# Expert tiles: each 128x128 transpose becomes two on the row halves of the array, in two PSUM banks, with the banks shared out anew

## The chip, the cores and the metric

The kernel runs on one core of a Trainium2 chip. The metric is the device time of one execution in microseconds (us). TensorE is called PE here (PEld is its weight load), VectorE DVE, ScalarE ACT, GpSimd POOL.

## The reference

Three layers follow one another, all in fp32:

```python
# 1. attention with a memory: B, H, S, D = 4, 8, 576, 64
x = (g * mem_out + (1 - g) * softmax(causal(q k^T / 8)) v)      # rows x become 2304 x 512
# 2. top-1 mixture of experts: E = 8, F = 1024
expert = argmax(x @ w_gate);  p = softmax(x @ w_gate)[expert]
x = p * (relu(x @ w1[expert]) @ w2[expert])                      # 512 -> 1024 -> 512
# 3. feed-forward layer
out = elu(x @ w_in) @ w_out                                      # 512 -> 2048 -> 512
```

## The kernel before

The program has three phases: attention, the expert tiles, and the last layer. In each phase operations are recorded in a plan (`Plan.op`, with a cost, a priority and what is read and written); `Plan.order` then simulates the engines with those costs and writes out a fixed order for each engine. So the order on the chip does not react to what really happens: each engine takes its instructions in the written order, and waits where one isn't ready.

Matmuls are done in fp32r, with each operand split into a high and a low part: three matmuls (high by high, low by high, high by low) stand for one. `split` makes the parts: a cast (`hi`, L1208 on ACT or L1211 on DVE) and a subtraction (`lo`, L1214 on DVE).

The expert phase (`moe`) works on tiles of 128 tokens, sorted by expert; 23 tiles run with this data. For each tile:

- the rows are gathered by a DMA of POOL (tile `xg` or `ex`, asked for early), and four transposes of 128x128 (L1277) put them with the features on the partitions, into one PSUM bank of ring `t`; every fourth column is taken (`sg.t[:, cc:DM:4]`). `split` makes `xh` and `xl` (or `x`, the same in the other buffer) from the bank. I call these four transposes an X group.
- 24 matmuls (L1337) with the first weights fill two banks of ring `g`, and two relus (L1347) empty them into `h`.
- two groups of four transposes (L1362), one for each half of `h`, go to two banks of ring `t`, and `split` makes `hh` and `hl` from each. These are the H groups.
- 24 matmuls (L1380) sum the tile's output in the bank of ring `y`; the result is scaled (L1393) and scattered to DRAM.

Two early tiles also have a group of transposes of their result (L1411, Y group). PSUM has eight banks: ring `g` has 4, `t` 3 and `y` 1. A bank of ring `t` is handed out again when the subtraction that reads it last (L1214) has ended.

When the next tile belongs to another expert, its weights must be split too: ACT casts 8 blocks of 128x1024 (L1313) and DVE subtracts 8 (L1318). These stand in every tile's order behind a branch on a flag (L1311, L1316), and are skipped where the expert stays the same. The plan gives them one cost (`m_if`, 700 ns for a pair) whether they are skipped or not. In the gaps, ACT and DVE also prepare the last layer's weights (L1127 on ACT; L1131, L1135, L1139, L1143 on DVE), with loads and stores of their own.

Of the kernel before, what the change touches and what calls it, by code (L numbers as in the profile page):

```python
# [18 lines left out]
P = 128  # L19
B, H, S, D = 4, 8, 576, 64  # L20
DM = H * D
# [59 lines left out]

class Op:
    __slots__ = ("eng", "cost", "fn", "prio", "lat", "need", "users", "slots", "ready", "start", "seq", "why", "dma", "lag", "waits", "dense", "span", "mode")


class Plan:
# [364 lines left out]
def ca(n, sb=False, bias=False, acc=False):  # L451
    if acc:
        return 240 + 0.833 * n
    return (110 if sb else 65) + 0.833 * n


def cv(n):
    return 70 + 1.04 * n


def cv2(n):
    return 75 + 0.52 * n
# [6 lines left out]
def cpt(n):  # L469
    return 150 + 2.1 * n  # L470
# [733 lines left out]
def split(c, src, hi, lo, n, rd, wh, wl, pr, psum, eh, el):  # L1204
    nc, pl = c.nc, c.pl

    def ha():
        nc.scalar.copy(hi(), src())  # L1208

    def hv():  # L1210
        nc.vector.tensor_copy(hi(), src())  # L1211

    def lv():
        nc.vector.tensor_sub(lo(), src(), hi().bitcast(F32))  # L1214

    def lp():
        nc.gpsimd.tensor_sub(lo(), src(), hi().bitcast(F32))
    he = {"ACT": (ca(n, sb=not psum), ha), "DVE": (cv(n) if psum else cv2(n), hv)}
    le = {"DVE": (cv(n), lv), "POOL": (cpt(n), lp)}
    for es, d, r, w in ((eh, he, rd, wh), (el, le, rd + [wh], wl)):  # L1220
        pl.op(es, [d[x][0] for x in es], [d[x][1] for x in es], r=r, w=[w], prio=pr)


def moe(tc, c, w1, w2, tiles):
    nc = tc.nc
    mp, pl, K = c.mp, c.pl, c.K
# [28 lines left out]
    def mtile(t):  # L1255
        pr = 1000.0 * t
# [3 lines left out]
        sg = Slot(r_xg)  # L1260
        if t:
            for j in range(2):
                if t == 1 and j == 1:

                    def f():
                        for w in raw[2:]:
                            nc.gpsimd.memset(w[0:1, 0:1], 0.0)
# [5 lines left out]
        wx, xh, xl = Slot(rt), Slot(r_xh), Slot(r_xl)  # L1273

        def f():
            for cc in range(4):
                nc.tensor.transpose(wx.t[:, cc * P:(cc + 1) * P], sg.t[:, cc:DM:4], c.ident)  # L1277
        if t:
            pl.op("PE", 436, f, r=[sg], w=[wx], prio=pr + K["m_x"])
        else:  # L1280
            xh.index, xl.index = r_xh.free.pop(0)[1], r_xl.free.pop(0)[1]
        for _ in range(t > 0):
            split(c, lambda: wx.t, lambda: xh.t.rearrange("p c n -> p (c n)"), lambda: xl.t.rearrange("p c n -> p (c n)"), 512,
                  [wx], xh, xl, pr + K["m_x"], True, K["xe"], ("DVE",))

        flags = {}
        for e, eng in (("ACT", mybir.EngineType.Activation), ("DVE", mybir.EngineType.DVE)) if t else ():
            def mk(e, eng):
                n = t - NE if part else t

                def f():
                    flags[e] = nc.values_load(c.R.sw[part][0:1, 1, n:n + 1], engines=[eng], min_val=0, max_val=1,
                                              skip_runtime_bounds_check_because="made on the chip as a flag")
                pl.op(e, 450, f, r=[("sw", part)], w=[("flag", e, t)], prio=pr + K["m_fl"])
# [29 lines left out]
        g = [Slot(rg), Slot(rg)]  # L1324
# [18 lines left out]
        sh = Slot(r_h)  # L1343
# [12 lines left out]
        for k in range(2):  # L1356
            def mk(k):
                wt, hh, hl = Slot(rt), Slot(r_hh), Slot(r_hl)

                def f():  # L1360
                    for j in range(4):
                        nc.tensor.transpose(wt.t[:, j * P:(j + 1) * P], sh.t[:, (4 * k + j) * P:(4 * k + j + 1) * P], c.ident)  # L1362
                pl.op("PE", 436, f, r=[(sh, k)], w=[wt], prio=pr + K["m_h"])
                split(c, lambda: wt.t, lambda: hh.t.rearrange("p c n -> p (c n)"), lambda: hl.t.rearrange("p c n -> p (c n)"), 512,
                      [wt], hh, hl, pr + K["m_h"], True, K["he"], ("DVE",))
                hs.append((hh, hl))
            mk(k)

        y, sy = Slot(ry), Slot(Ring("last", [c.wraw[0][0][:, 2 * XW:3 * XW]]) if t == NTM - 1 else r_y)
# [34 lines left out]
        if t < NE:  # L1404
            wy = Slot(rt)
            n = P * (t - NE + NY)
            yh, yl = [lambda x=x: c.y0.t[:, x, 4 * n:4 * (n + P)] for x in range(2)]

            def f():
                for cc in range(4):  # L1410
                    nc.tensor.transpose(wy.t[:, cc * P:(cc + 1) * P], sy.t[:, cc * P:(cc + 1) * P], c.ident)  # L1411
            pl.op("PE", 436, f, r=[sy, "y0"], w=[wy], prio=pr + 500)
            split(c, lambda: wy.t, yh, yl, 512, [wy], ("yh", n), ("yl", n), pr + 500, True,
                  K["he"], ("DVE",))
            return

# [10 lines left out]
    for t in tiles:  # L1427
        mtile(t)
# [217 lines left out]
def kernel(ctx, tc, q, k, v, M_prev, z_prev, beta, w_gate, w1, w2, w_in, w_out, out):  # L1646
    nc = tc.nc
    c = Ctx()
# [8 lines left out]
    def psum(stack, name, n, two=0):  # L1657
        pp = stack.enter_context(tc.tile_pool(name=name, bufs=1, space=bass.MemoryType.PSUM))
        return [pp.tile([P, 512], F32, name=f"{name}{i}") for i in range(n)], [pp.tile([P, 1024], F32, name=f"{name}t{i}") for i in range(two)]
# [30 lines left out]
    with ExitStack() as s1:  # L1690
        c.wraw = [[wp.tile([P, 2048], F32, name=f"wraw{i}", tag=f"wraw{i}") for i in range(4)]]
        ep = s1.enter_context(tc.tile_pool(name="ep", bufs=1))
        c.x0 = [ep.tile([P, 4, P], F32R, name=f"x0{i}") for i in range(2)]
        c.wq = [[ep.tile([P, 1024], F32R, name=f"wq{n}{i}") for i in range(2)] for n in range(1)]
        with ExitStack() as s2:
            c.ap = s2.enter_context(tc.tile_pool(name="ap", bufs=1))
            c.qone = c.ap.tile([P, NI, 2 * QH], BF16, name="qone")
            c.ap.tile([P, (-8800 % LINE) // 4], F32, name="apad")
            nx = c.K["rings"]
            banks, twos = psum(s2, "pa", 8 - 2 * nx, nx)  # L1700
            c.rx = Ring("x", twos)
            c.rw = Ring("w", banks) if banks else c.rx
            c.rs = c.rw

            def build():
                constants(tc, ctx, c, M_prev, z_prev, beta, w_gate)
                attention(tc, ctx, c, q, k, v, M_prev)
                routing(tc, c, c.rw, True, c.K["early"])
                for j in range(2):
                    tile_weights(tc, c, (w1, w2), 0, j, prio=c.K["early"], dma=5830)  # L1710
                gather(tc, c, 0, lambda: c.ex[:, 0:XW], r=[("tok", 0)] + [("xd", b) for b in range(B - 1)], w=[c.se], prio=c.K["early"])
                first_parts(c)
                n, t0, dt = c.K["warm"]
                keep_busy(c, c.rw, [t0 + dt * i for i in range(n)], 1.0e8)
                wd = Widen.inside(tc, c, w_in, w_out)
                for n in range(c.K["wa"]):
                    wd.part(n, c.K["wa0"] + c.K["wa1"] * n)
            phase(build, c.K["sa"], 0.0, POOL=3000.0, DVE=1800.0, ACT=500.0, PE=2000.0)
        with ExitStack() as s2:
            c.mt = {}  # L1720
            c.mp = s2.enter_context(tc.tile_pool(name="mp", bufs=1))
            c.qone = c.mp.tile([P, NI, 2 * QH], BF16, name="qone")
            c.mp.tile([P, (-1440 % LINE) // 4], F32, name="mpad")
            c.wraw.append([c.mp.tile([P, 2048], F32, name=f"wrbw{i}") for i in range(4)])
            banks, _ = psum(s2, "pm", 8)
            c.rg, c.rt, c.ry = Ring("g", banks[:4]), Ring("t", banks[4:7]), Ring("y", banks[7:])
            
            def build():
                c.wd = Widen.inside(tc, c, w_in, w_out)
                keep_busy(c, c.rg, [0.0] * c.K["busy"][1], -1.0e8)  # L1730
                c.gate(c.rt, c.K["late"])
                routing(tc, c, c.rt, False, c.K["late"])
                moe(tc, c, w1, w2, range(NTM))
                for i, n in enumerate(range(c.K["wa"], 4 * NS)):
                    c.wd.part(n, 1.0e7 + 1.0e4 * i, r=[("tile", c.K["wt"] + int(i * c.K["wq"]))])
            phase(build, c.K["sm"])

            nt = nc.values_load(c.R.nt[0:1, 0:1], min_val=0, max_val=NT, skip_runtime_bounds_check_because="made on the chip as a count of tiles")
            with tc.If(nt > NTM):
                phase(lambda: moe(tc, c, w1, w2, range(NTM, NT)), c.K["sm"])  # L1740
    with ExitStack() as s1:
        c.tp = s1.enter_context(tc.tile_pool(name="tp", bufs=1))
        banks, _ = psum(s1, "pt", 8)
# [35 lines left out]
```

## Time and profile before

| | |
|---|---|
| median of 3 runs | 955.74 us (953.25 to 956.02) |
| profiled execution | 954.44 us, its span 952.7 us |
| PE busy in the span | 921.3 us (97%) |
| DVE, ACT, POOL busy | 639.2, 446.9, 179.6 us |
| granted clock of PE, mean | 0.991 |
| attention, experts, last layer | 0 to about 243, to 538, to 953 us |

A matmul's record is longer than the time it costs, since matmuls overlap in the array: "390 ns" of a matmul with 512 columns says little, while the distance from its start to the start of the next one, 0.23 us, is its price where PE is the bound. All prices of PE below are such distances.

### The profile page before, as it was taken

The numbers are of one execution on the slowest core, as the hardware profiler recorded it, in microseconds if no ns is written. First come the engines' busy times: TensorE is split into PE (matmuls) and PEld (weight loads), VectorE is DVE, ScalarE is ACT, GpSimd is POOL, SyncE is SP. The second block draws the span as 40 slices with busy tenths as digits, with TensorE's granted clock in tenths as the row PEclk, the third lists the DMA queues.
The fourth block names the chain that finished last, engine by engine and source line by source line (L and its number), as shares of the span: only waits on it lengthen the run. The fifth ranks groups of instructions, "written<-read, shape, count | busy, mean of one in ns | idle before, by whom it ended". The sixth has DMA issues, their size and how long they took to land. (4 is left out here: it accounts for less than half of the span.)

```text
span 952.7 us, 18441 instructions
## 1 busy us (share of the span) xinstructions
PE 921.3 (97%) x6858; PEld 770.3 (81%) x6858; DVE 639.2 (67%) x1179; ACT 446.9 (47%) x902; POOL 179.6 (19%) x244
## 2 busy tenths in 40 slices
PE   9998998999899999999999999999999999999996
PEld 6777887778678888888878789988888888888895
DVE  3878878887775568646898596555565556555553
ACT  3787778767454347536866562222122221212211
POOL 3344442434300122222321100010001000100100
PEclk8999999989999999999999999999999999999999
DMA  6333433243632697569997370110011000100000
GB/s 124 79 75 84 94 75 103 64 147 132 221 122 88 228 343 250 170 225 361 331 335 279 125 242 1 34 45 1 1 45 45 1 12 23 45 0 1 20 26 23
DMA packets 96597, 110.00 MB, mean 115 GB/s; under 512 B 64879, under 2 KB 64879, under 8 KB 94193
## 3 DMA queue, kind: packets, MB, share of 16 engines
q1 hardware_dynamic: 90496, 95.25, 31.4%
q0 software_dynamic: 4800, 13.18, 3.8%
q8 instruction: 55, 0.90, 0.4%
q10 hardware_dynamic: 1200, 0.30, 0.2%
q14 instruction: 46, 0.37, 0.1%
HBM read 87.94 MB, written 23.41 MB: 117 GB/s over the span
## 5 line engine op out<-in xcount | busy, mean ns | idle before, releaser
L1588 ACT ACTIVATE elu<-pt 128x512 f32<-128x512 f32 x72 | 43.1, 598 | 266.0 <-PE pt L1580 266.0
L1613 PE MATMUL pt<-w,gh 128*128 128x512 f32 x432 | 134.2, 392 | 0.5 <-DVE gh L1492 0.5
L1380 PE MATMUL pm<-w,hh 128*128 128x512 f32 x368 | 125.1, 401 | 0.8 <-ACT y L1393 0.8
L1596 DVE TENSOR_SCALAR elu<-elu 128x512 f32<-128x512 f32 x72 | 30.8, 428 | 127.1 <-ACT elu L1588 127.1
L1613 PEld LDWEIGHTS pt<-w,gh 128*128 128x128 f32 x432 | 79.6, 188 | 16.3 <-DVE gh L1492 0.9
L692 ACT ACTIVATE a<-pat,st 128x128 f32<-128x128 f32 (+2 forms) x144 | 78.0, 550 | 22.5 <-DVE st L687 18.3
L1613 PE MATMUL pt<-w,gl 128*128 128x512 f32 x216 | 84.3, 390 | 0.0
L1380 PEld LDWEIGHTS pm<-w,hh 128*128 128x128 f32 x368 | 69.2, 188 | 14.5 <-ACT y L1393 1.2
L1380 PE MATMUL pm<-w,hl 128*128 128x512 f32 x184 | 71.9, 391 | 0.3 <-DVE hl L1214 0.3
L687 DVE TENSOR_REDUCE st<-pat 128x2 f32<-128x256 f32 (+4 forms) x80 | 63.8, 806 | 9.6 <-PE pat L671 9.6
L1580 PE MATMUL pt<-yTh,w 128*128 128x256 f32 (+1 forms) x288 | 69.2, 319 | 0.0
L705 PE MATMUL pat<-ident,a 128*128 128x128 f32 x400 | 56.9, 287 | 8.6 <-ACT a L692 8.4
L628 POOL TENSOR_SCALAR ex<-ex 128x512 f32<-128x512 f32 (+1 forms) x32 | 37.8, 1182 | 131.0 <-ACT ex L604 118.5
L705 PEld LDWEIGHTS pat<-ident,a 128*128 128x128 f32 x400 | 44.6, 145 | 16.0 <-ACT a L692 15.0
L1600 DVE SCALAR_TENSOR_TENSOR tnh<-tnh,elu 128x512 f32<-128x512 f32 x72 | 49.6, 690 | 7.7 <-ACT tnh L1592 1.8
L1337 PE MATMUL pm<-w,x 128*128 128x512 f32 x216 | 51.9, 392 | 1.3 <-DVE w L1214 0.9
L1495 DVE TENSOR_TENSOR gl<-tnh,gh 128x512 fp32r<-128x512 f32 x72 | 49.6, 691 | 4.2
L1580 PEld LDWEIGHTS pt<-yTh,w 128*128 128x128 f32 x288 | 49.2, 190 | 4.0
L1604 DVE SCALAR_TENSOR_TENSOR tnh<-pt,tnh 128x512 f32<-128x512 f32 x72 | 49.6, 690 | 3.3
L1337 PEld LDWEIGHTS pm<-w,x 128*128 128x128 f32 x216 | 40.2, 188 | 10.3 <-DVE w L1214 1.4
L1214 DVE TENSOR_TENSOR hl<-pm,hh 128x512 fp32r<-128x512 f32 x46 | 31.4, 684 | 25.0 <-ACTq L1311 14.4
L1613 PEld LDWEIGHTS pt<-w,gl 128*128 128x128 f32 x216 | 40.5, 188 | 9.0 <-DVE gl L1495 0.4
(342 smaller groups left out, 2107.3 us busy)
## 6 DMA issues: line engine op xcount, KB each, us to landing
wraw<-in_moe_w_dram SPq DMA_DIRECT2D x24, 1024.0 KB, 7.9
wrbw<-in_moe_w_dram SPq DMA_DIRECT2D x12, 1024.0 KB, 8.1
wide<-in_moe_w_in_dram SPq DMA_DIRECT2D x16, 512.0 KB, 5.4
wf<-half SPq DMA_DIRECT2D x32, 256.0 KB, 3.2
wide<-in_moe_w_out_dram SPq DMA_DIRECT2D x16, 512.0 KB, 5.8
wide<-wf SPq DMA_DIRECT2D x9, 512.0 KB, 5.3
q<-in_q_dram SPq DMA_DIRECT2D x32, 128.0 KB, 3.1
v<-in_v_dram SPq DMA_DIRECT2D x32, 128.0 KB, 2.5
```

The lines of the kernel that those rows point to most:

```text
L628: nc.gpsimd.tensor_scalar(e, e, 1.0, 0.0, op0=ALU.min, op1=ALU.add)
L687: nc.vector.tensor_reduce(ss.t[:, 2 * i:2 * i + (2 if i < 4 else 1)], src(), axis=AX.X if i < 4 else AX.XY, op=ALU.min)
L692: nc.scalar.activation(sa[i].t[:, h, :] if i < 4 else sa[4].t[:, 0:S].rearrange("p (y n) -> p y n", y=2), src()[:, h, :] if i < 4 else src ...
L705: nc.tensor.transpose(w.t[:, y:y + P], t[:, j * P:(j + 1) * P], c.ident)
L1337: nc.tensor.matmul(g[hf].t, a.t[:, cc, :], b[:, 512 * hf:512 * (hf + 1)], start=(cc == 0 and n == 0), stop=(cc == 3 and n == 2))
L1380: nc.tensor.matmul(y.t, a.t[:, 2 * (q % 2) + jj, :], b[:, 512 * jj:512 * (jj + 1)], start=(q == 0 and jj == 0 and n == 0), stop=(q == 3 an ...
L1495: nc.vector.tensor_sub(lo(), src(), hi().bitcast(F32))
L1580: nc.tensor.matmul(h.t[:, n * j + n0:n * j + n1], w(cc, a, ft), b(cc), start=(cc == 0 and x == 0), stop=(cc == 3 and x == 2))
L1588: nc.scalar.activation(se.t, h.t, AF.Exp)
L1600: nc.vector.scalar_tensor_tensor(st.t, st.t, 0.0, se.t, op0=ALU.min, op1=ALU.mult)
L1604: nc.vector.scalar_tensor_tensor(st.t, h.t, 0.0, st.t, op0=ALU.max, op1=ALU.add)
L1613: nc.tensor.matmul(acc[a].t, y.t[:, n * j + P * a:n * j + P * (a + 1)], wsub(1, k, ft // 2)[:, ft % 2, :], start=(ft == 0 and x == 0), sto ...
```

## The change

Each transpose of 128x128 in the expert phase becomes two: the upper 64 rows of the source with the upper left 64x64 corner of the identity, and the lower 64 with the lower right corner. Each gives 128 partitions by 64 columns; the upper halves go to one bank and the lower halves to a second, so that a group of four becomes eight transposes and takes a pair of banks. `split` reads the pair through an access pattern that puts the columns together again. The cost in the plan falls from 436 to 8 x 33 = 264 ns for a group. Ring `g` now has 3 single banks, `t` two pairs, `y` 1 bank. Attention (L1194 too) and the last layer keep their transposes.

```diff
+TURN = 33
+
+def turn(nc, out, x, ident, n):
+    for y in range(n):
+        for z in range(2):
+            zs = slice(z * D, (z + 1) * D)
+            nc.tensor.transpose(out[:, 512 * z + D * y:512 * z + D * (y + 1)], x(y)[zs], ident[zs, zs])
+
+def turned(w, n):
+    return w.rearrange("p (z x) -> p z x", z=2)[:, :, 0:n * D].rearrange("p z (c q) -> p c z q", q=D)
+
+def halved(t):
+    return t.rearrange("p c (z q) -> p c z q", z=2)
...
         def f():
-            for cc in range(4):
-                nc.tensor.transpose(wx.t[:, cc * P:(cc + 1) * P], sg.t[:, cc:DM:4], c.ident)
+            turn(nc, wx.t, lambda cc: sg.t[:, cc:DM:4], c.ident, 4)
         if t:
-            pl.op("PE", 436, f, r=[sg], w=[wx], prio=pr + K["m_x"])
+            pl.op("PE", 8 * TURN, f, r=[sg], w=[wx], prio=pr + K["m_x"])
...
                 def f():
-                    for j in range(4):
-                        nc.tensor.transpose(wt.t[:, j * P:(j + 1) * P], sh.t[:, (4 * k + j) * P:(4 * k + j + 1) * P], c.ident)
-                pl.op("PE", 436, f, r=[(sh, k)], w=[wt], prio=pr + K["m_h"])
+                    turn(nc, wt.t, lambda j: sh.t[:, (4 * k + j) * P:(4 * k + j + 1) * P], c.ident, 4)
+                pl.op("PE", 8 * TURN, f, r=[(sh, k)], w=[wt], prio=pr + K["m_h"])
+                split(c, lambda: turned(wt.t, 4), lambda: halved(hh.t), lambda: halved(hl.t), 512, [wt], hh, hl, pr + K["m_h"], True, K["he"], ("DVE",))
...
-            banks, _ = psum(s2, "pm", 8)
-            c.rg, c.rt, c.ry = Ring("g", banks[:4]), Ring("t", banks[4:7]), Ring("y", banks[7:])
+            banks, twos = psum(s2, "pm", 4, 2)
+            c.rg, c.rt, c.ry = Ring("g", banks[:3]), Ring("t", twos), Ring("y", banks[3:])
```

The plan's order moves with the costs and the rings. Two places of one tile show how; it is a tile with a change of expert, which starts its X group at 473.70 us of the execution before. First PE, before: the X group, the first H group, then three matmuls L1380, and the second H group into the third bank (`pm4`, `pm5`, `pm6` are the banks of ring `t`).

```order
L1277 MATMUL pm6_3722<-ident_98,xg2_3750 128x128 [waits DMASW6_49]
L1277 MATMUL pm6_3722<-ident_98,xg2_3750 128x128 x3
L1362 MATMUL pm4_3720<-ident_98,h0_3724 128x128 [waits Activation_49]
L1362 MATMUL pm4_3720<-ident_98,h0_3724 128x128 x3
L1380 MATMUL pm7_3723<-w40_3738,hh1_3727 128x512
L1311 UNCONDITIONAL_BRANCH
L1380 MATMUL pm7_3723<-w40_3738,hl1_3730 128x512
L1380 MATMUL pm7_3723<-w41_3739,hh1_3727 128x512 [waits DVE_49]
L1362 MATMUL pm5_3721<-ident_98,h0_3724 128x128 [waits Activation_49]
L1362 MATMUL pm5_3721<-ident_98,h0_3724 128x128
```

The same place with the change; L94 is the line of the transposes in `turn`, L1395 is what L1380 was, `pmt0` and `pmt1` are the two pairs.

```order
L94 MATMUL pmt1_3721<-ident_98,xg2_3748 128x64 [waits DMASW6_49]
L94 MATMUL pmt1_3721<-ident_98,xg2_3748 128x64 x7
L94 MATMUL pmt0_3720<-ident_98,h0_3722 128x64 [waits DVE_49,Activation_49]
L94 MATMUL pmt0_3720<-ident_98,h0_3722 128x64 x7
...
L1395 MATMUL pm3_3719<-w41_3737,hh1_3725 128x512
L1395 MATMUL pm3_3719<-w50_3734,hh1_3725 128x512
L1395 MATMUL pm3_3719<-w50_3734,hl1_3728 128x512
L1395 MATMUL pm3_3719<-w51_3735,hh1_3725 128x512 [waits DVE_49]
L94 MATMUL pmt0_3720<-ident_98,h0_3722 128x64 [waits DVE_49]
L94 MATMUL pmt0_3720<-ident_98,h0_3722 128x64 x7
L1395 MATMUL pm3_3719<-w50_3734,hh1_3725 128x512
```

The second H group has moved from behind three matmuls to behind nine, it goes into the pair that the first H group had, and its wait is now for DVE, which must have made `hl` from the first.

Second, DVE in the same tile, before: the weights' pair (L1318, taken here), the last step of the preparation (L1143), then `xl` and `hl`; the three other steps of the preparation stand ahead of these rows.

```order
L1318 TENSOR_TENSOR wq01_85<-wrbw0_3709,wq00_84 128x1024 [waits DMAHW3_49,DMAHW1_49,DMAHW7_49,PE_49,Activation_49]
L1318 TENSOR_TENSOR w11_3745<-wrbw0_3709,w10_3744 128x1024 [waits PE_49,Activation_49]
L1316 UNCONDITIONAL_BRANCH
L1316 UNCONDITIONAL_BRANCH [waits DVE_49]
L1143 SCALAR_TENSOR_TENSOR half_73<-wide0_71,half_73 128x512 [waits DVE_49]
L1311 UNCONDITIONAL_BRANCH
L1214 TENSOR_TENSOR xl0_3747<-pm6_3722,xh0_3746 128x512 [waits Activation_49]
L1214 TENSOR_TENSOR hl0_3729<-pm4_3720,hh0_3726 128x512 [waits Activation_49]
```

And with the change (L1335 was L1318, L1150 to L1158 were L1131 to L1139, L1230 is a cast of `split` on DVE, L1233 was L1214):

```order
L1335 TENSOR_TENSOR wq01_85<-wrbw0_3709,wq00_84 128x1024 [waits DMAHW3_49,DMAHW1_49,DMAHW7_49,PE_49,Activation_49]
L1335 TENSOR_TENSOR w11_3743<-wrbw0_3709,w10_3742 128x1024 [waits PE_49,Activation_49]
L1333 UNCONDITIONAL_BRANCH
L1333 UNCONDITIONAL_BRANCH [waits DVE_49]
L1150 TENSOR_SCALAR half_73<-half_73 128x512 [waits Activation_49]
L1154 TENSOR_SCALAR half_73<-half_73 128x512 [waits DVE_49]
L1158 SCALAR_TENSOR_TENSOR half_73<-wide0_71,half_73 128x512 [waits DMAHW2_49,DVE_49]
L1230 CAST xh0_3744<-pmt1_3721 128x512 [waits PE_49]
L1328 UNCONDITIONAL_BRANCH
L1233 TENSOR_TENSOR hl0_3727<-pmt0_3720,hh0_3724 128x512 [waits Activation_49]
L1233 TENSOR_TENSOR xl0_3745<-pmt1_3721,xh0_3744 128x512 [waits DVE_49]
```

Three preparation steps have moved between the weights' pair and `hl`, and the cast `xh`, which ACT made before, is now DVE's. That is so in 16 of the 22 X groups.

## Rows read from the trace of the kernel before

**Rows 1.** The page: busy time of each engine, with its share of the span.

```profile
PE 921.3 (97%) x6858; PEld 770.3 (81%) x6858; DVE 639.2 (67%) x1179; ACT 446.9 (47%) x902; POOL 179.6 (19%) x244
```

**Rows 2.** Windows: length, PE, PEld, DVE, ACT, POOL busy, clock, DMA.

```profile
375.00:400.00 25.00, 25.00 (x124) 21.02 (x123) 19.39 (x30) 12.99 (x20) 5.24 (x6) 1.00 0.51 166
475.00:500.00 25.00, 24.05 (x116) 19.89 (x114) 23.80 (x32) 17.25 (x25) 5.09 (x6) 1.00 0.93 333
```

**Rows 3.** Timeline of PE in an ordinary tile: start, length, line, operation, count.

```profile
337.94 0.63 PE L1277 MATMUL pm<-ident,ex 128*128 128x128 f32 x4
338.40 0.60 PE L1362 MATMUL pm<-ident,h 128*128 128x128 f32 x4
...
339.31 0.39 PE L1380 MATMUL pm<-w,hh 128*128 128x512 f32 x1
339.54 0.60 PE L1362 MATMUL pm<-ident,h 128*128 128x128 f32 x4
339.89 0.48 PE L1380 MATMUL pm<-w,hh 128*128 128x512 f32 x1
340.21 0.39 PE L1380 MATMUL pm<-w,hl 128*128 128x512 f32 x1
```

**Rows 4.** Timeline of PE in attention, where operations of half the array stand.

```profile
80.39 0.75 PE L570 MATMUL pat<-ident,q 128*128 128x128 f32 x5
81.07 0.86 PE L529 MATMUL pat<-mb,qpT 64*64 64x73 f32 x40
81.75 0.81 PE L529 MATMUL pat<-iw,xT 64*64 64x72 f32 x40
...
102.64 0.26 PE L671 MATMUL pat<-mask,id 64*128 64x128 bf16 x4
102.73 0.94 PE L667 MATMUL pat<-ab 64*128 64x512 f32 x6
103.52 0.26 PE L671 MATMUL pat<-mask,id 64*128 64x128 bf16 x4
103.71 1.06 PE L678 MATMUL pat<-ab 128*128 128x288 f32 x6
```

**Rows 5.** Weight loads of the transposes: duration in ns, min/median/max.

```profile
L1277 PEld LDWEIGHTS pm<-ident,xg x68: 195/208/215, 251.9 to 512.4; 128*128 128x128 f32 x68
L1362 PEld LDWEIGHTS pm<-ident,h x184: 138/140/156, 250.8 to 526.3; 128*128 128x128 f32 x184
```

**Rows 6.** Timeline of DVE in the ordinary tile.

```profile
339.24 0.69 DVE L1214 TENSOR_TENSOR x<-pm,x 128x512 fp32r<-128x512 f32 x1 [2.01 <-ACT x L1208]
```

**Rows 7.** Line L1318: the first weight block of each change of expert.

```profile
L1318 DVE TENSOR_TENSOR wq<-wraw,wq x5: 1212/1223/1225, 263.1 to 512.3; 128x1024 fp32r<-128x1024 f32 x5
L1318 DVE TENSOR_TENSOR wq<-wrbw,wq x3: 1211/1218/1218, 348.3 to 475.1; 128x1024 fp32r<-128x1024 f32 x3
```

**Rows 8.** Timeline of PE and DVE in a tile with a change of expert.

```profile
473.59 0.42 DVE L1131 TENSOR_SCALAR half<-half 128x512 f32<-128x512 f32 x1
...
474.17 0.62 PE L1362 MATMUL pm<-ident,h 128*128 128x128 f32 x4
...
475.11 1.22 DVE L1318 TENSOR_TENSOR wq<-wrbw,wq 128x1024 fp32r<-128x1024 f32 x1
...
477.38 0.68 DVE L1143 SCALAR_TENSOR_TENSOR half<-wide,half 128x512 uint32<-128x512 uint32 x1
477.98 0.68 DVE L1214 TENSOR_TENSOR xl<-pm,xh 128x512 fp32r<-128x512 f32 x1
478.58 0.68 DVE L1214 TENSOR_TENSOR hl<-pm,hh 128x512 fp32r<-128x512 f32 x1
```

**Rows 9.** The same in an earlier tile with a change of expert.

```profile
363.23 1.22 DVE L1318 TENSOR_TENSOR w<-wraw,w 128x1024 fp32r<-128x1024 f32 x1
...
363.54 0.66 PE L1362 MATMUL pm<-ident,h 128*128 128x128 f32 x4 [0.41 <-ACT h L1347]
```

More of the change, by code (lines that the diff above doesn't have):

```diff
@@ L1282, in mtile @@
         for _ in range(t > 0):
-            split(c, lambda: wx.t, lambda: xh.t.rearrange("p c n -> p (c n)"), lambda: xl.t.rearrange("p c n -> p (c n)"), 512,
-                  [wx], xh, xl, pr + K["m_x"], True, K["xe"], ("DVE",))
+            split(c, lambda: turned(wx.t, 4), lambda: halved(xh.t), lambda: halved(xl.t), 512, [wx], xh, xl, pr + K["m_x"], True, K["xe"], ("DVE",))
         flags = {}
@@ L1360, in f @@
                 def f():
-                    for j in range(4):
-                        nc.tensor.transpose(wt.t[:, j * P:(j + 1) * P], sh.t[:, (4 * k + j) * P:(4 * k + j + 1) * P], c.ident)
-                pl.op("PE", 436, f, r=[(sh, k)], w=[wt], prio=pr + K["m_h"])
-                split(c, lambda: wt.t, lambda: hh.t.rearrange("p c n -> p (c n)"), lambda: hl.t.rearrange("p c n -> p (c n)"), 512,
-                      [wt], hh, hl, pr + K["m_h"], True, K["he"], ("DVE",))
+                    turn(nc, wt.t, lambda j: sh.t[:, (4 * k + j) * P:(4 * k + j + 1) * P], c.ident, 4)
+                pl.op("PE", 8 * TURN, f, r=[(sh, k)], w=[wt], prio=pr + K["m_h"])
+                split(c, lambda: turned(wt.t, 4), lambda: halved(hh.t), lambda: halved(hl.t), 512, [wt], hh, hl, pr + K["m_h"], True, K["he"], ("DVE",))
                 hs.append((hh, hl))
@@ L1406, in mtile @@
             n = P * (t - NE + NY)
-            yh, yl = [lambda x=x: c.y0.t[:, x, 4 * n:4 * (n + P)] for x in range(2)]
+            yh, yl = [lambda x=x: c.y0.t[:, x, 4 * n:4 * (n + P)].rearrange("p (c z q) -> p c z q", z=2, q=D) for x in range(2)]
             def f():
[L1410 to L1413, printed above, removed]
+                turn(nc, wy.t, lambda cc: sy.t[:, cc * P:(cc + 1) * P], c.ident, 4)
+            pl.op("PE", 8 * TURN, f, r=[sy, "y0"], w=[wy], prio=pr + 500)
+            split(c, lambda: turned(wy.t, 4), yh, yl, 512, [wy], ("yh", n), ("yl", n), pr + 500, True,
                   K["he"], ("DVE",))
```

## The prediction

> **What bounds the kernel now.** I read the page first: PE is busy 97% of the span [rows 1]. That is an average, so I went on to the windows of the expert phase. PE is busy for the whole of a 25 us window in the middle of it, at full clock, while DVE is busy 19.4 us and ACT 13.0 [rows 2]. Late in the phase the picture shifts: between 475 and 500 us PE has lost 1 us, and DVE is at 23.8 of 25 [rows 2]. So what the expert phase costs is PE's time from start to start, plus whatever PE has to wait for. The last layer starts when the expert tiles are done, and PE is the bound there as well, so a saving or a loss in the expert phase goes through to the end one to one. That is why I priced transposes by distances on PE's timeline, and then looked at DVE, which gives the banks back.
>
> **The price of a group before.** The X group starts at 337.94 and the next group at 338.40: 0.46 us [rows 3]. For an H group take the stretch behind it: normal matmuls stand 0.23 apart (339.31 to 339.54); the H group takes 0.35 (339.54 to 339.89), and the matmul after it stands 0.32 from its successor, 0.09 more than normal. So an H group costs 0.44 [rows 3]. With 23 tiles, of which the first gets its X group in attention, there are 22 X groups, 46 H groups and 2 Y groups (priced as H): 22 x 0.46 + 48 x 0.44 = 31.2 us. That is all this change can work on.
>
> **The price of a group after, while it streams.** No half transposes stand in the expert phase before, but attention has work on parts of the array. Forty fp32 matmuls on quarters (64*64) with 73 columns start 0.68 us apart from the next forty, 17 ns each, so four of them go in 68 ns [rows 4]. Four quarters are two row halves over the whole width, which is just a pair of half transposes; with 64 columns in place of 73 the pair costs 0.068 x 64/73 = 0.060 us, and four pairs 0.24. Row halves with 512 columns agree that they overlap: six matmuls in 0.79 us (102.73 to 103.52), 0.13 each, against the 0.23 of a full one [rows 3, 4]. So I take 0.24 for an H group, down from 0.44.
>
> The X group is another matter. Its weight load takes 208 ns, that of H 140 [rows 5]; the source is read with a step of four elements. Its transposes stand 0.46/4 = 0.115 apart [rows 3]. A half transpose loads 64 rows but still 128 columns with the same step. If the step is what makes the load slow, a pair costs 0.115, and the X group stays at 0.46; if the two halves were free of it, 0.24. I take 0.46, the group's own row.
>
> **What the change adds on PE.** Every time PE goes from full-array to half-array work, or back, it pays. Back: a block of L671 on halves is followed by other half work after 0.09 us (102.64 to 102.73) and by full work after 0.19 (103.52 to 103.71): 0.10 us more [rows 4]. There: five full transposes ahead of quarter work take 0.68 us (80.39 to 81.07), where their own pace, (0.75 - 0.28)/4 = 0.12 with about 0.28 for a single record, makes 0.59: 0.09 more [rows 4]. So a block of neighbouring groups costs 0.19 on top, however many groups are in it. [...]
>
> In the new order the 70 groups that run form 51 blocks (45 before): an X group usually shares its block with the first H group, and the second H group stands alone between matmuls. 51 x 0.19 = 9.7 us.
>
> The sum on PE: 22 x 0.46 + 48 x 0.24 + 9.7 = 10.1 + 11.5 + 9.7 = 31.3 us, against 31.2. The halving gains 9.6 us and the changes of mode take them back: 0.1, which I call nothing. The ends: with X also at 0.24 it is -4.7; with changes of mode free as well, -14.4; if the halves did not overlap at all, H would stay at 0.44 and the sum be +9.7.
>
> **What the change adds in waits.** Ring `t` had three banks, so the second H group never waited for its own tile's splits. Now there are two pairs and three groups per tile. The second H group needs the pair of the X group or of the first H group, and so DVE's subtraction from it. In an ordinary tile that is harmless: the last L1214 on X starts 1.3 us after the X group began and lasts 0.69 [rows 3, 6], while the new order puts nine matmuls, 9 x 0.23 = 2.1 us, between the two H groups. In a tile with a change of expert DVE is late, because the weights' blocks, 1.22 us each, stand in its queue, and the plan has them at a fraction of that. There are 5 + 3 = 8 such changes [rows 7].
>
> Take the tile at 474 us [rows 8]. The first H group starts at 474.17. In the new order the second has its turn 0.24 + 0.10 + 9 x 0.23 + 0.09 later, at 476.7. DVE meanwhile: the weights' pair takes 477.38 - 475.11 = 2.3 us, the three preparation steps 475.11 - 473.59 = 1.5, the new cast and `hl` 0.6 each (477.98 to 478.58). From 473.59 that ends at 478.6. PE waits 1.9 us with all of the tile's output matmuls queued behind. In the tile at 363 the H group starts at 363.54, so its second turn is at 366.0; DVE starts the pair's second block at 363.23 and is done after 1.1 us, and then come four short operations and the subtraction that frees the pair, 0.45 + 0.45 + 3 x 0.6 in the new order: 366.6 [rows 8, 9]. That is a wait of 0.6. The 16 casts that move from ACT to DVE add 0.6 each to a DVE with little left to give late in the phase [rows 2]. On the other hand, each wait lets DVE catch up before the next. For the eight changes I take half the mean of the two, (1.9 + 0.6)/4 = 0.63 us each, 5.0 in all. The ends are nothing and 8 x 1.9 = 15.
>
> Edits at no cost: ring `g` with three banks is hidden, since a tile needs two and the relus that free them have the 24 matmuls L1380 (24 x 0.23 = 5.5 us) to end in; without that cover it would cost a relu per tile. Reading a pair of banks moves as many elements as before, so I leave casts and subtractions at their length. The gathers, the scatters, the weights' loads and the last layer are untouched.
>
> **The sum**, on the profiled execution's 954.4 us: 954.4 + 0.1 + 5.0 = 959.5. That execution lies 1.3 below the median of the runs, 955.7, from which the same sum is 960.8; I say **960.0 us**, between the two.
>
> **The rivals.**
> - *Faster, about 950.* The X group streams like the H groups (-4.7), and the waits come to 1 us or less because the new order moves preparation steps out of the way: 954.4 - 4.7 + 1 = 950.7. For it: in most tiles DVE has room, and quarter work ran at 17 ns apiece. Against it: DVE at 23.8 of 25 [rows 2], and the 208 ns load [rows 5]. It decides, X at 0.24 given, once the waits stay under 3.2 us in total (954.4 - 4.7 + 3.2 = 952.9). Chance 0.23.
> - *No change, 953 to 958.* Modes and halves cancel on PE, and the waits are 1 to 3 us. For it: the sum on PE is nothing already. Against it: one tile alone makes 1.9. Chance 0.25.
> - *The change doesn't halve anything, about 967.* If loading 128 columns sets the pace of a half transpose as it sets that of X, an H group stays at 0.44 and the changes of mode come on top: 954.4 + 9.7 + 3 (a slower PE waits less) = 967. Against it: 140 ns against 208 in the loads [rows 5], and the overlap in attention [rows 4]. Chance 0.09. [...]
> - *The forecast, slower by the waits for DVE, 958.6 to 968.* Chance 0.43.
>
> **How the numbers follow.** A measurement of this kernel can tell about 0.3% from no change, which is 2.9 us: below 952.9 is faster, above 958.6 slower. The chances are those of the cases: 0.23 faster, 0.25 within, 0.43 + 0.09 = 0.52 slower. The time is that of the likeliest case, 960.0, whose own range is 957 to 967; the range for all reaches down to the faster rival, 950, and up to the third, 968.
>
> **What the profile of the changed kernel would show.** The halving: eight half transposes of H within 0.24 us of PE's timeline, and some 0.1 us extra on either side of a block. The X group: eight in 0.46, not 0.24. The waits: PE idle ahead of the second H group with DVE's `hl` or `xl` as what ended it, 0.5 to 2 us at each change of expert and none in ordinary tiles; DVE with 16 casts of `x` or `xh` that ACT had. The prediction is wrong if ordinary tiles come out clearly shorter than before (then modes or X cost less than I say), or if PE does not wait at the changes of expert.

## The result: 966.33 us, slower by 1.2%, and the profile after

The changed kernel took 966.33 us (median of 4 runs, 965.0 to 968.13), the kernel before 955.16 beside it: a ratio of 1.0121, 95% interval 1.0096 to 1.0145. The prediction was 960.0 (950 to 968): the direction was right, the movement 11.2 us where its sum had 5.1 (0.1 on PE and 5.0 of waits). The profiled execution has a span of 963.9 us.

The page gives the busy time of each engine. PE has 280 records more and 8 us more of busy time than in [rows 1]; DVE has the 17 casts that ACT gave up.

```profile
PE 929.6 (96%) x7138; PEld 762.4 (79%) x7138; DVE 649.5 (67%) x1196; ACT 441.4 (46%) x885; POOL 184.4 (19%) x244
```

The windows of the changed kernel (columns as in [rows 2]), with one from the start of the expert phase added. PE is still the bound in the middle, and DVE is no fuller late in the phase than before (22.59 for 23.80). At the start the granted clock is 0.93; before (first row), it was 1.00 in that window. The last row is the stretch that makes the difference: the granted clock is 0.50 in its 3.4 us, and 21.6 us at 1.00 with 3.4 at 0.50 make 0.93.

```profile
250.00:275.00 25.00, 23.05 (x141) 18.25 (x140) 19.94 (x62) 13.00 (x23) 1.19 (x3) 1.00 0.74 267
```

```profile
250.00:275.00 25.00, 22.05 (x144) 17.41 (x144) 17.55 (x58) 10.81 (x19) 0.00 (x0) 0.93 0.65 235
...
375.00:400.00 25.00, 25.00 (x143) 19.47 (x142) 19.75 (x27) 14.31 (x20) 6.77 (x6) 1.00 0.50 153
475.00:500.00 25.00, 24.42 (x142) 19.28 (x141) 22.59 (x28) 18.45 (x25) 5.67 (x6) 1.00 0.86 300
...
252.70:256.10 3.40, 3.40 (x15) 2.71 (x16) 3.30 (x7) 0.69 (x2) 0.00 (x0) 0.50 0.96 343
```

PE's timeline of the changed kernel: the start, an ordinary tile (against [rows 3]), a tile with a change of expert (against [rows 8]), and the hand-over to the last layer. L1354 and L1395 are the old L1337 and L1380, L94 the half transposes, L1594 the last layer's first product.

```profile
251.08 0.69 PE L94 MATMUL pmt<-ident,xg 64*128 64x64 f32 x8 [1.20 <-DVE hl L1233]
...
253.86 0.63 PE L1395 MATMUL pm<-w,hl 128*128 128x512 f32 x1
254.29 0.63 PE L1395 MATMUL pm<-w,hh 128*128 128x512 f32 x1
...
284.86 0.50 PE L1354 MATMUL pm<-wq,xl 128*128 128x512 f32 x1 [0.63 <-DVE xl L1233]
...
342.07 0.39 PE L1354 MATMUL pm<-w,xh 128*128 128x512 f32 x1
342.39 0.69 PE L94 MATMUL pmt<-ident,ex 64*128 64x64 f32 x8
342.92 0.41 PE L94 MATMUL pmt<-ident,h 64*128 64x64 f32 x8
343.26 0.50 PE L1395 MATMUL pm<-w,hh 128*128 128x512 f32 x1
343.60 0.39 PE L1395 MATMUL pm<-w,hl 128*128 128x512 f32 x1
343.83 0.62 PE L1395 MATMUL pm<-w,hh 128*128 128x512 f32 x2
...
345.21 0.39 PE L1395 MATMUL pm<-w,hh 128*128 128x512 f32 x1
345.53 0.46 PE L94 MATMUL pmt<-ident,h 64*128 64x64 f32 x8
345.92 0.50 PE L1395 MATMUL pm<-w,hh 128*128 128x512 f32 x1
346.26 0.39 PE L1395 MATMUL pm<-w,hl 128*128 128x512 f32 x1
346.49 0.63 PE L1395 MATMUL pm<-w,hh 128*128 128x512 f32 x2
...
485.68 0.46 PE L94 MATMUL pmt<-ident,h 64*128 64x64 f32 x8 [0.58 <-DVE hl L1233]
...
546.15 0.39 PE L1395 MATMUL pm<-w,hh 128*128 128x512 f32 x1
549.13 2.44 PE L1594 MATMUL pt<-raw1n,raw0n 128*128 128x256 f32 x12 [2.59 <-DVEq L1753]
```

Read starts, not lengths. Normal matmuls stand 0.23 apart. From the matmul ahead of the lone H block (345.21) to the third behind it (346.49) are 1.28 us; three normal distances are 0.69, so the block costs **0.59**. In its parts: 0.32 into the block (0.09 too much), 0.39 from the first half to the next matmul, and 0.34 from that matmul to its successor (0.11 too much). The block of X and the first H group costs 343.83 - 342.07 - 0.69 = 1.07. Before, the same reading gave 0.44 or 0.45 and 0.92.

The time from a tile's first L1354 to the next tile's, worked out from all starts, says where the 11.2 us went. An ordinary tile takes 12.60 us for 12.28. The first four tiles take 56.5 for 51.4, and the hand-over to the last layer (546.15 to 549.13) 3.0 for 1.2. The tiles with changes of expert late in the phase (18 to 21, counted from 0) take 51.4 for 51.2. The sum over the expert phase is 305.0 for 294.4. Attention, which is not touched, ended 2 us earlier in this execution (it ends between 241.2 and 243.8 us in all runs told of here), and the last layer was 0.9 longer.

The waits of PE, changed kernel (columns: what waited, for what; us, times, longest), and one row of the kernel before:

```profile
PE pt L1594 <- DVEq L1753: 2.6, 1, 2.6
PE pmt L94 <- DVE hl L1233: 1.8, 2, 1.2
```

```profile
PE pm L1362 <- ACT h L1347: 1.8, 4, 0.9
```

The forecast wait for DVE's `hl` is there twice, 1.2 us at the start and 0.6 at one change of expert, not at eight. And a wait that the prediction had not priced is nearly gone: before, H groups stood 1.8 us for ACT's relus, now 0.2 (one H group). That ACT has 17 casts less fits this; no run tests it.

### The profile page after: what moved, and what is told of

It is laid out like the page before. It is cut to its first block, busy times and chain, and to the rows that moved or that the text cites. A ratio compares the mean times of both kernels' runs of the same rounds, so it can differ in the third digit from the quotient of the medians.

```text
span 963.9 us, 18982 instructions
## 1 busy us (share of the span) xinstructions
PE 929.6 (96%) x7138; PEld 762.4 (79%) x7138; DVE 649.5 (67%) x1196; ACT 441.4 (46%) x885; POOL 184.4 (19%) x244
## 5 line engine op out<-in xcount | busy, mean ns | idle before, releaser
L1395 PE MATMUL pm<-w,hh 128*128 128x512 f32 x368 | 129.1, 408 | 1.0 <-ACT y L1408 1.0
L1395 PEld LDWEIGHTS pm<-w,hh 128*128 128x128 f32 x368 | 69.2, 188 | 18.2 <-ACT y L1408 1.4
L1395 PE MATMUL pm<-w,hl 128*128 128x512 f32 x184 | 72.2, 392 | 0.0
L1594 PE MATMUL pt<-yTh,w 128*128 128x256 f32 (+1 forms) x288 | 69.2, 319 | 0.0
L724 PE MATMUL pat<-ident,a 128*128 128x128 f32 x400 | 54.9, 280 | 9.2 <-ACT a L711 8.8
L1614 DVE SCALAR_TENSOR_TENSOR tnh<-tnh,elu 128x512 f32<-128x512 f32 x72 | 49.6, 691 | 6.8 <-ACT tnh L1606 0.9
L1354 PE MATMUL pm<-w,x 128*128 128x512 f32 x216 | 51.8, 392 | 1.2 <-DVE w L1233 0.9
L1594 PEld LDWEIGHTS pt<-yTh,w 128*128 128x128 f32 x288 | 49.2, 190 | 3.9
L1354 PEld LDWEIGHTS pm<-w,x 128*128 128x128 f32 x216 | 40.2, 188 | 10.4 <-DVE w L1233 1.4
L1202 POOL DMA_INDIRECT xg<-xd,r_tok x17 | 21.3, 1252 | 133.1 <-ACTq L1328 101.5
```

The lines of the kernel that those rows point to most:

```text
L724: nc.tensor.transpose(w.t[:, y:y + P], t[:, j * P:(j + 1) * P], c.ident)
L1354: nc.tensor.matmul(g[hf].t, a.t[:, cc, :], b[:, 512 * hf:512 * (hf + 1)], start=(cc == 0 and n == 0), stop=(cc == 3 and n == 2))
L1395: nc.tensor.matmul(y.t, a.t[:, 2 * (q % 2) + jj, :], b[:, 512 * jj:512 * (jj + 1)], start=(q == 0 and jj == 0 and n == 0), stop=(q == 3 an ...
L1594: nc.tensor.matmul(h.t[:, n * j + n0:n * j + n1], w(cc, a, ft), b(cc), start=(cc == 0 and x == 0), stop=(cc == 3 and x == 2))
L1614: nc.vector.scalar_tensor_tensor(st.t, st.t, 0.0, se.t, op0=ALU.min, op1=ALU.mult)
```

## The experiments

**Theories.** *Blocks:* each block of halves pays a fixed price for the two changes of mode (from full-array to half-array work and back), more than the 0.19 us of the prediction, and that makes most of the loss. *Rings:* two pairs for three banks make it. *Halves:* a half transpose is slow in itself. The first four runs keep the changed kernel's rings and order, and change only which groups are halves.

**All transposes full, into the first bank of each pair.**

```diff
-            turn(nc, wx.t, lambda cc: sg.t[:, cc:DM:4], c.ident, 4)
+            [nc.tensor.transpose(wx.t[:, cc * P:(cc + 1) * P], sg.t[:, cc:DM:4], c.ident) for cc in range(4)]
```
(likewise for H and Y; the splits read `[:, 0:512]`)

> The changed kernel's rings (three single banks, two pairs, one) and its order on every engine, but every transpose full again, into the first bank of its pair. If the price is paid for the two mode changes around each block (the lone second block of a tile 0.59 us in the changed kernel for 0.44 before, the block of X and the first H group 1.07 for 0.90), an ordinary tile falls from 12.60 to about 12.28 us, the whole by about 46 blocks x 0.16 = 7 us, to about 959; what stays over the 955 of before is what the rings cost at the start of the expert phase and at its end. If the loss comes from having two pairs for three single banks, it stays: 964 to 967, tiles at 12.6.

Measured: 959.2 us, ratio 1.0056 (1.0039 to 1.0073). An ordinary tile is back at 12.27 to 12.34 us (12.28 before). So the halves cost 966.33 - 959.2 = 7.1 us, or 6.2 by the two ratios, and the rings with the order 4 to 5.

**H and Y groups in halves, X full.**

```diff
-            turn(nc, wx.t, lambda cc: sg.t[:, cc:DM:4], c.ident, 4)
+            [nc.tensor.transpose(...) for cc in range(4)]      # X alone
```

> Rings and order of the changed kernel; X groups full, H and Y groups in halves. Price by blocks (streams 0.235 for eight halves, 0.09 into the block, 0.10 out, 0.11 more on the matmul behind it, in all 0.535 for an H group in halves against 0.44): above the kernel with all transposes full by 46 x 0.1 = 4.5 us, and below the changed kernel by 22 x 0.07 = 1.5, so about 964.5. Price by halves, the same for each group of eight: two thirds of the loss, also about 964. Rings: 964 to 967. This run tells apart only together with the one that has X alone in halves.

Measured: 966.01 us, ratio 1.0117 (1.0100 to 1.0134); the profiled execution itself took 969.97, so only distances are read from it. An ordinary tile takes 12.63. Over the run with all full that is 6.8 us where 4.5 were expected: a lone H group in halves stands at 0.59 or 0.60 for 0.44, 0.15 more and not 0.1.

**X groups in halves, H and Y full.** The opposite edit.

> Rings and order of the changed kernel; X groups in halves, H and Y groups full. Price by blocks: there are still 22 blocks with mode changes (0.30 each) and X's halves take 0.53 for 0.46, so 22 x 0.37 = +8 us over the kernel with all transposes full, about 967: taking the halves from two thirds of the groups gives nothing back. Price by halves: a third of the loss, about 961.5. Rings: no difference to the kernel with all full.

Measured: 966.75 us, ratio 1.0131 (1.0115 to 1.0148); an ordinary tile 12.62. A third of the groups in halves costs as much as all of them. Of the three theories only the price by blocks gives that.

**One half transpose behind each H group, otherwise all full.**

```diff
+ nc.tensor.transpose(wt.t[:, 512:512 + D], sh.t[0:D, 512 * k:512 * k + P], c.ident[0:D, 0:D])
```

> As the kernel with all transposes full in pairs, but behind each H group one half transpose (64 rows) is added, into the second bank of the pair, where nobody reads it: 44 mode changes there and back with almost no work between. Price by blocks: 0.09 + 0.06 + 0.10 + 0.11 = 0.36 each, 44 x 0.36 = +16 us over that kernel, about 975. If a mode change costs only 0.19 there and back, as the prediction had it, 44 x 0.25 = +11. If mode changes cost next to nothing and halves are what is slow, 44 x 0.06 = +2.6.

Measured: 976.23 us, ratio 1.0226 (1.0208 to 1.0244): 17.0 us over the kernel with all full. There are 46 H groups, not the 44 that I wrote, so 0.37 each. PE's timelines, lone H group, first all full, then with the one half:

```profile
355.44 0.39 PE L1395 MATMUL pm<-w,hh 128*128 128x512 f32 x1
355.67 0.60 PE L1378 MATMUL pmt<-ident,h 128*128 128x128 f32 x4
356.03 0.47 PE L1395 MATMUL pm<-w,hh 128*128 128x512 f32 x1
356.34 0.39 PE L1395 MATMUL pm<-w,hl 128*128 128x512 f32 x1
```

```profile
362.08 0.39 PE L1395 MATMUL pm<-w,hh 128*128 128x512 f32 x1
362.32 0.80 PE L1378 MATMUL pmt<-ident,h 128*128 128x128 f32 x5
363.05 0.50 PE L1395 MATMUL pm<-w,hh 128*128 128x512 f32 x1
363.38 0.39 PE L1395 MATMUL pm<-w,hl 128*128 128x512 f32 x1
```

From the first transpose to the next matmul 0.36 became 0.73: one half, where a pair of them streams in 0.06, costs 0.37. The distance behind that matmul is 0.31 after full transposes already, and 0.33 to 0.34 after halves.

**Every H group's eight halves issued twice** (the second set writes the same again).

```diff
-                    turn(nc, wt.t, lambda j: sh.t[...], c.ident, 4)
+                    turn(nc, wt.t, lambda j: sh.t[...], c.ident, 4); turn(nc, wt.t, lambda j: sh.t[...], c.ident, 4)
```

> The changed kernel with the eight half transposes of every H group issued twice over, in the same block: 44 x 8 more halves, no more mode changes. Price by blocks: only the stream is added, four pairs of 0.058 = 0.235 us a group, 44 x 0.235 = +10.3 us, about 976.6. [...] If halves hide wholly behind weight loads, no more than +2.

Measured: 976.71 us, ratio 1.0236 (1.0221 to 1.0252), 10.4 over the changed kernel. Sixteen halves take 0.65 to the next matmul, eight took 0.39: 0.25 for eight more, where the first eight cost 0.59 as a block.

```profile
362.62 0.71 PE L94 MATMUL pmt<-ident,h 64*128 64x64 f32 x16
363.27 0.50 PE L1395 MATMUL pm<-w,hh 128*128 128x512 f32 x1
```

So halves do stream at the forecast pace. A half loads 128 columns as a full transpose does, and the record of its load is as long (139 ns, below, for 140 in [rows 5]). But the record does not set the pace: in H's blocks of the changed kernel the two loads of a pair start 4 ns apart, and the next pair follows after 0.06 us, where the full transposes of the kernel before follow each other after 0.109.

**X groups read consecutive columns.** The first layer's weight rows are loaded in the order that fits.

```diff
-            turn(nc, wx.t, lambda cc: sg.t[:, cc:DM:4], c.ident, 4)
+            turn(nc, wx.t, lambda cc: sg.t[:, cc * P:(cc + 1) * P], c.ident, 4)
-  src.rearrange("o (p h c) f -> h p (o c f)", p=P, h=2) if j == 0
+  src.rearrange("o (h c p) f -> h p (o c) f", p=P, h=2) if j == 0
...
```

> The changed kernel, but the X groups read 128 consecutive columns instead of every fourth; the first layer's weight rows are loaded in the order that fits (two runs of 4 KB for a partition instead of one of 8 KB), so that the result is unchanged. If the strided read is what keeps X's halves at 0.116 us a pair where H's take 0.058, 22 groups gain 4 x 0.058 = 0.23 each, 5.1 us: about 961, an ordinary tile 12.37. If the pace of X's halves comes from something else (their place at the block's start, the mode change), no change: 966.

Measured: 964.02 us, ratio 1.0099 (1.0083 to 1.0114), and an ordinary tile 12.39 where 12.37 was expected. The tile moved as forecast, the whole by less (2.3 of 5.1). In the profiled executions the expert phase is 3.7 us shorter, 301.2 for 305.0; the rest lies in attention and the last layer, where only the first tile's X group was changed. Weight loads of the half transposes, changed kernel and this one (ns, min/median/max):

```profile
L94 PEld LDWEIGHTS pmt<-ident,h x368: 134/139/159, 248.7 to 534.4; 64*128 64x128 f32 x184
...
L94 PEld LDWEIGHTS pmt<-ident,xg x136: 192/215/220, 251.1 to 520.7; 64*128 64x128 f32 x136
```

```profile
L94 PEld LDWEIGHTS pmt<-ident,xg x136: 134/139/226, 253.0 to 518.2; 64*128 64x128 f32 x136
```

The step of four elements is the whole difference: 215 becomes 139, which is H's figure. On PE's timeline X's eight halves take 0.30 us to the H group behind them (355.40 to 355.70), for 0.53 with the step (342.39 to 342.92).

**Full transposes, and `g` with its four banks back, the transposes with two single ones.**

```diff
...
+  c.rg, c.rt, c.ry = Ring("g", banks[:4]), Ring("t", banks[4:6]), Ring("y", banks[6:])
```

> All transposes full, as in the kernel with full ones in pairs, in the same order, but the rings are four single banks for g, two single ones for the transposes, one for y: g has its old number back, the transposes still have two. If the 4 to 5 us that remain over before come from two buffers for the transposes (the stops of 1.0 us at the start of the expert phase), it stays at about 959; if they come from g's three, it falls to 955.

Measured: 958.85 us, ratio 1.0049 (1.0035 to 1.0063). `g`'s bank is worth nothing, as forecast. What is left over the kernel before goes with two transpose buffers and with the order that the plan makes for them; no run separates the two. The order is that of the run with all full, and PE stands 1.01 us for `hl`, whose subtraction frees a buffer, at the first X group, and 1.01 for `xl`, an operand, at the fourth tile, as it does there:

```profile
253.33 0.75 PE L1295 MATMUL pm<-ident,xg 128*128 128x128 f32 x4 [1.01 <-DVE hl L1233]
...
284.95 0.50 PE L1354 MATMUL pm<-wq,xl 128*128 128x512 f32 x1 [1.01 <-DVE xl L1233]
```

Its first four tiles take 53.8 us for 51.4 before, its hand-over 2.3 for 1.2.

**One block a tile.** From tile 3 on the next tile's X group and both H groups (in one pair) are one block; before that, the two H groups are. Columns are consecutive, and the plan now takes 30 ns for a half and 320 for a block, so its order moves again.

```diff
...
+        def f():
+            if nxt:
+                nxt[9]()                      # X group of tile t + 1
+            for k in range(2):
+                turn(nc, wt.t[:, 256 * k:], lambda j: sh.t[...], c.ident, 4)
```

> Consecutive columns as in the run on the strided read, and from the fourth tile on one block of halves a tile: the next tile's X group and both H groups together (both H groups share one pair), in place of two or three blocks. Price by blocks: 0.595 for a block of eight halves and 0.235 for each further eight, 1.06 a tile, for 0.83 + 0.595 = 1.43 with two blocks: 18 x 0.37 = 6.7 us less than the run on the strided read, about 954 to 955, an ordinary tile 11.97 us for 12.28 before. Price by halves: the same number of halves, so no change to that run, 961. Ring: the waits at the start stay, and both H groups now wait for the second rectifier, which the six second-layer steps ahead of the block should cover.

Measured: 957.68 us, ratio 1.0035 (1.0021 to 1.0049), where 954 to 955 were expected. The ordinary tile takes 11.99 us, 0.29 less than before:

```profile
352.28 0.39 PE L1416 MATMUL pm<-w,hh 128*128 128x512 f32 x1
352.60 0.46 PE L95 MATMUL pmt<-ident,xg 64*128 64x64 f32 x8
352.89 0.66 PE L95 MATMUL pmt<-ident,h 64*128 64x64 f32 x16
353.49 0.50 PE L1416 MATMUL pm<-w,hh 128*128 128x512 f32 x1
353.82 0.40 PE L1416 MATMUL pm<-w,hl 128*128 128x512 f32 x1
354.06 0.62 PE L1416 MATMUL pm<-w,hh 128*128 128x512 f32 x2
```

24 halves cost 354.06 - 352.28 - 0.69 = 1.09 us, where two blocks of full transposes cost 1.37 before. The first three tiles give 3.8 us back (43.0 for 39.2; the granted clock from 250 to 275 us is 0.86 there, for 0.93 in the changed kernel and 1.00 before), the last two 2.7.

**Before with consecutive columns**, as a base.

> The kernel before, rings and full transposes and order unchanged, but X groups read consecutive columns (the first layer's weight rows loaded in the order that fits). A full transpose of strided columns takes 0.12 us and of consecutive ones 0.109, so 22 x 4 x 0.011 = 1 us less: within 0.3% of before. It is the base for the run with one block and four banks: what that gains more comes from the block.

Measured: 954.0 us, ratio 0.9997 (0.9981 to 1.0013). An ordinary tile takes 12.25 us, so the block alone is worth 0.26 a tile.

**One block, and the four banks as one ring of singles.** Tiles 0 to 2 and the last tile have full transposes.

```diff
...
+  Ring("t", [c.four[:, 512 * i:512 * (i + 1)] for i in range(4)])   # c.four: one tile of four banks
```

> One block of halves a tile as in the run with one block, but the four banks of the two pairs are one ring of single banks: tiles 0 to 2, the tables of the routing, the Y groups and the last tile use single banks and full transposes, and from tile 3 on X takes two of the four banks and the two H groups the other two. If the block's price (ordinary tile 11.99 for 12.28, some 17 tiles, -5 us) and the lack of a third buffer at the start and the end (+4 to +6 in the run with one block) are what made 957.7, this run gives 950 to 952. If what that run lost is the later second rectifier and the x cast that comes behind DVE's weight work at expert changes (8 of them, up to 1 us each, and 3 us at the last), it stays at 955 or above.

Measured: 976.12 us, ratio 1.0221 (1.0196 to 1.0246), a miss. Ordinary tiles are at 11.99 here too, but the first three take 49.6 (39.2 before), tiles 18 to 21 57.8 (51.2) and the last two 36.2 (30.9). In the first tile the second H group waits for the split of the first (0.68 us, 252.04), though it has a bank of its own:

```profile
250.71 0.66 PE L100 MATMUL pmt<-ident,h 128*128 128x128 f32 x4
252.04 0.66 PE L100 MATMUL pmt<-ident,h 128*128 128x128 f32 x4 [0.68 <-ACT hh L1239]
254.69 0.66 PE L100 MATMUL pmt<-ident,xg 128*128 128x128 f32 x4 [2.00 <-DVEq L1363]
```

These four banks were one tile of the program; that its parts then wait for each other is my reading, not tested.

**One block, `g` with two banks, a single bank for X and Y groups at the start.** These groups, and the H groups of tiles 0 to 2 and of the last tile, are full transposes.

```diff
...
+  c.rg, c.rt, c.ry, c.r1 = Ring("g", banks[:2]), Ring("t", twos), Ring("y", banks[3:]), Ring("s", banks[2:3])
```

> One block of halves a tile from tile 3 on, as in the run with one block, but with other buffers: g has two single banks, one single bank is for the X groups of tiles 1 to 3 and the Y groups (full transposes), the two pairs are for the routing, for the two H groups of tiles 0 to 2 and of the last tile (full, one pair each) and from tile 3 on for X and for both H groups. So the start has its third transpose buffer again, in separate banks. If the missing third buffer made the stops at the start (1 to 1.7 us at X groups, with half clock behind them), the first three tiles come back to about 39 to 40 us together (39.2 before, 43.0 in the run with one block), the last two to 31 to 32, and the whole is 951 to 953. If g needs its third bank, or the stops have another cause, it stays at 957 or above.

Measured: 955.57 us, ratio 1.0005 (0.9990 to 1.0020). The whole misses the 951 to 953 that were expected. The first three tiles take 39.8, as expected, and the first X group no longer waits. But they also went back to full transposes, and with those and two buffers (the run with all full) they take 40.1; so most of what the run with one block lost there, 43.0, is not shown to be the third buffer's. Ordinary tiles stay at 11.99, so `g` does with two banks. The last two take 33.7 for 30.9, behind a wait for the cast of X:

```profile
514.44 0.39 PE L1434 MATMUL pm<-w,hh 128*128 128x512 f32 x1
516.10 0.50 PE L1378 MATMUL pm<-wq,x 128*128 128x512 f32 x1 [1.27 <-DVE x L1236]
```

**The same, the last tile's X group not joined.**

```diff
-        nxt = xpart(t + 1, True) if JOIN <= t and t + 1 in tiles else None
+        nxt = xpart(t + 1, True) if JOIN <= t < NTM - 2 else None
```

> As the run with g in two banks, but the last tile's X group is no longer joined to the block of the tile ahead of it; it goes full, into the single bank, early, as before. There the cast of X came behind DVE's weight work of an expert change and the last two tiles took 33.7 us for 30.9. If that wait is what ate the block's gain, the last two tiles come back to about 31 us and the whole is 953 to 954, 0.2% under before. If the wait moves on to the next thing that DVE does late, it stays at 955.6.

Measured: 957.28 us, ratio 1.0026 (1.0013 to 1.0038), where 953 to 954 were expected. The wait moved on, as its second case said, and grew: the last two tiles take 36.6.

```profile
523.65 0.50 PE L1434 MATMUL pm<-w,hh 128*128 128x512 f32 x1 [1.95 <-ACTq L1352]
...
525.89 0.90 PE L104 MATMUL pmt<-ident,h 128*128 128x128 f32 x3 [1.28 <-ACT h L1388]
```

So no version here beats the kernel before; the best ties with it.

## Why the prediction was off

- **The price of a block is the step that failed**: "So a block of neighbouring groups costs 0.19 on top", 51 x 0.19 = 9.7, and with it the sum on PE, "0.1, which I call nothing". Both parts that it had are confirmed: 0.09 into the block, and 0.10 back (342.92 to 343.26 is 0.34, of which 0.24 are the stream). Two were left out. The matmul behind the block stands 0.11 late to its successor; the prediction read its price before up to that second matmul (0.35 + 0.09), its price after only up to the first. And the first pair of a block takes 0.05 more than the others (eight halves of H take 0.39 to the next matmul alone, 0.34 behind X's). So a block costs 0.09 + 0.05 + 0.10 + 0.11 = 0.35 where 0.19 were put, 51 x 0.35 = 17.9 us.
- **H streaming at 0.24**: right, by the run with the halves twice (0.25). **X at its old pace, 0.46**: right (0.53 to the next group, with the first pair's 0.05), and the strided load is the reason (0.30 with consecutive columns).
- **The sum on PE** with the measured terms: 22 x 0.46 + 48 x 0.24 + 17.9 = 39.5, against 22 x 0.47 + 48 x 0.45 = 31.9 before: +7.6 for the +0.1 forecast. Between the changed kernel and the one with all full the runs show 6.2 to 7.1, and the expert phases of the two profiles 305.0 - 297.0 = 8.0. Of these 8.0, 2.7 lie in the first four tiles (56.5 for 53.8); at 0.3 a tile the halves would make 1.2 there. The other 1.5 fits the stretch at the lower clock, which the run with all full doesn't have (an estimate: 3.4 us at half pace lose 1.7).
- **Waits, +5.0 at eight changes of expert**: the size is about what the run with all full leaves over before (4 to 5 us in two runs), but the place is wrong, so that the size fits is luck. Only one change shows such a wait, 0.58 us where I had 1.9 for that tile. In the run with all full 2.4 us lie in the first four tiles, with two stops of 1.0 us, one for a buffer and one for an operand; in the changed kernel the first is 1.2, and a stretch at a granted clock of 0.50 follows it and some short groups (252.7 to 256.1; matmuls 0.43 apart from 253.86 on, 0.23 otherwise). What brings that stretch is open: the run with all full stops 1.01 us at the same group, and its clock is 1.00 in that window. The waits for relus fell by 1.6 us when casts left ACT; I had priced that move on DVE only. And one sum is off: in the tile at 363 the terms 363.23 + 1.1 + 0.45 + 0.45 + 3 x 0.6 make 367.0 and not 366.6, a wait of 1.0 for 0.6, and 5.8 in all for the 5.0.
- **The hand-over**, +1.8 us, was in no term. In the other runs in this order it is 1.0 to 1.2 more than before, 0.1 in one of them; it is 0.1 more in three of the four runs with one block and 2.0 in that with four banks as one ring. The runs with full transposes have it too, so the halves don't make it. The trace shows what is late. The last layer begins when DVE has done its last step of the phase, a subtraction for the last layer's first weights; before, that was over by 536.65, ahead of the last expert matmul (537.62). Now ACT's cast for it stands 4.1 us for the load, which SyncE issues at 542.08 (before: 521.34), and the subtraction ends at 548.93. PE starts at 549.13. Why the load comes so late was not tested.

```profile
535.43 1.22 DVE L1214 TENSOR_TENSOR wraw2n<-wide,wraw2n 128x1024 fp32r<-128x1024 f32 x1
```

```profile
546.62 1.04 ACT L1227 CAST wraw2n<-wide 128x1024 fp32r<-128x1024 f32 x1 [4.10 <-DMA wide<-wf]
...
547.70 1.23 DVE L1233 TENSOR_TENSOR wraw2n<-wide,wraw2n 128x1024 fp32r<-128x1024 f32 x1 [1.29 <-SPq L1753]
```

- **Ring `g` at no cost**: shown, by three, four and two banks.
- **Rivals.** "The change doesn't halve anything" had the right time, 967, for the wrong reason: the halves overlap, a pair every 0.06 us. Nor do the 128 columns set X's pace, as that rival has it; the step does (0.53 against 0.30 us). The record of a load of half the rows is as long as that of a full one (139 ns for 140); the pace of H's pairs doesn't follow that record.

## What to carry to other kernels

Price an edit from the matmul ahead of a block to the second behind it, in the old form and in the new alike. Half-array transposes save 0.20 us a group here and cost 0.35 a block, so by these prices two groups in a block are about the break-even, and three gain: 0.26 a tile in the run with one block (11.99 us for 12.25 with full transposes, both with consecutive columns). A buffer that ordinary tiles never miss can be missed at the start of a phase (1.20 us at the first X group here), and a new order can leave work late at its end (a load issued at 542.08 for 521.34): look at both first when a ring shrinks.

## What the hardware showed that I had not expected

One half transpose behind four full ones costs 0.37 us, more than three full ones (0.109 us apart). The runs give this price; what PE does in that time no row shows. And two half transposes with a load record of 139 ns each start a pair every 0.06 us, where full ones with 140 ns start every 0.109.
